# First MoE in eleven items of 384 tokens with singles and pairs between them

## The chip, the core and the metric

The kernel runs on one core of a Trainium2 chip, in one launch. The metric is the device time of one execution in microseconds. Three runs of the kernel before gave 1198.8, 1201.47 and 1198.43 us, a median of 1198.8. The engines are TensorE (PE; its weight loads PEld), VectorE (DVE), ScalarE (ACT), GpSimd (POOL) and SyncE (SP), which here issues most DMAs.

## The reference

Three steps follow one another: attention with keys and values averaged over groups of eight, a mixture of eight experts in which each of 4608 tokens goes to one of them, and a gated product without routing.

```python
scores = scale * np.matmul(q, k_p.transpose(0, 1, 3, 2))     # 8 x 8 heads, 576 queries, 72 pooled keys
x = softmax(scores) @ v_p                                    # as (4608, 512)
expert_idx = np.argmax(xn @ en.T / tau, axis=1)              # first MoE: one of E = 8 experts for a token
for e in range(E):
    mask = expert_idx == e
    h = np.maximum(x[mask] @ w1[e], 0.0)                     # 512 -> 1024
    out[mask] = gate_w[mask, None] * (h @ w2[e])             # 1024 -> 512
h = np.maximum(np.maximum(x @ m1, x @ m2), x @ m3)           # second MoE: 512 -> 768
return h @ mo                                                # 768 -> 512
```

The inputs are drawn with a fixed seed, so the routing is the same in every run.

## The kernel before

Attention takes the span up to about 166 us. The first MoE follows to 661 us. It sorts tokens by expert into blocks of 128, and works in *items*: a pair is two blocks of one expert, a single is one block. There are 18 pairs, of which the first `NE` are taken from the first 24 tiles of tokens while attention still runs, then the singles, of which four always run; more run only behind a branch on a number that the routing leaves in `nsing`. `run()` (L1525) goes through the items in turn, each in eight steps `p_`. Steps 0 to 3 are `mm1` (L1154): 256 of the 1024 hidden columns each, x times w1, with relu into `hhi` (ACT) and `hlo` (DVE). Steps 4 to 7 are `mm2` (L1191): the products with w2 gather in the four quarters of `py`. Every fp32 product is done as three matmuls of rounded parts: high x high, high x low, low x high. A weight piece, `w1raw` or `w2raw`, is split by `split()` two steps ahead of its use: ACT writes `whi`, DVE writes `wlo`; right after it the piece of the next item is loaded into the same buffer, skipped if the expert is the same. In mm1 a single takes fp32 products of 128 columns on unsplit weights; in mm2 its h is the stationary side, against 512 columns.

The next item's tokens are gathered by POOL into `xrow`, one indirect DMA for each block, in step 0. In step 5 `transpose_x` (L1112) turns them by TensorE into `px`, from where ACT copies `xhi` and DVE takes the rest as `xlo`. `px` comes from the pool `pq` with two PSUM banks. At the end of an item ACT copies `py` to `yo`, and SP stores it in `ybuf`.

Every engine takes its instructions in the order in which the program issues them. `between()` (L1564) is called twice in a step and issues, next to the item's own work, small steps of the routing (`fill`), then `conversions` (the raw weights of the second MoE turned to fp32 in `mraw`, through `cvraw` and `cvy`) and `combinations` (sums of weight blocks `wsum`, split into `wst`, stored by POOL to `wdram`, nine blocks in all), both mostly on DVE and ACT. The second MoE, from 661 us, reads these sums and works in groups of 768 tokens in the order of `ybuf`, with matmuls of 384 columns (L1901) on banks of PSUM.

The lines on which the order around the change rests:

```python
if p_ == 0 and i + 1 in items:
    gather(i + 1)
if p_ == 5 and i + 1 in items:
    transpose_x(i + 1)
```

## Time and profile before

| what | value |
|---|---|
| median of three runs | 1198.8 us |
| profiled execution, its own time | 1199.76 us |
| span of its trace | 1198.0 us |
| busy share of the span: TensorE, VectorE, ScalarE, GpSimd | 98%, 73%, 51%, 25% |
| DMA, mean over the span | 238 GB/s |

The span runs from the first to the last instruction in the trace. Busy time of TensorE counts overlapping matmuls once, and the end of a matmul is modelled: the time from one start to the next tells how fast it streams, better than the length of one. A wait is the idle time of an engine before an instruction, with the instruction that released it. [...]

### The profile page before, as it was taken

Reading aid. Unit: us, or ns where it says so; the run is one execution under the profiler, and the core shown is the slowest. Engines: PE = TensorE matmul, PEld = TensorE weight load, DVE = VectorE, ACT = ScalarE, POOL = GpSimd, SP = SyncE. Lnnn points to the kernel's source line nnn. Section 1 sums busy time; section 2 is a strip of 40 time slices with the busy share of each in tenths; the row PEclk is TensorE's granted clock in tenths of the full one; section 3 lists DMA queues with packets and bytes.
Section 4 is the critical chain, followed back from the end, with each engine's and each line's share of the span. In section 5 each row is a group of like instructions: output and inputs, shape, how many; then the busy total and the mean of one; then the engine's idle time right before and its main releaser. Section 6 shows DMA issues by size and latency. Waiting matters only on the chain.

```text
span 1198.0 us, 24005 instructions
## 1 busy us (share of the span) xinstructions
PE 1179.1 (98%) x8829; PEld 1165.6 (97%) x8829; DVE 876.7 (73%) x1811; ACT 607.2 (51%) x1117; POOL 302.9 (25%) x471
## 2 busy tenths in 40 slices
PE   8999999999999999999999999999999999999997
PEld 8999899999999999999999999999999999999997
DVE  7888977977899899988765468467557557567563
ACT  4676665455676666666655334334334334334332
POOL 8876843001212121221101202103004004004001
PEclk9999999999999999999999999999999999999999
DMA  9979665328865447554939677877878877877873
GB/s 287 314 194 257 182 213 189 102 24 262 269 230 201 148 169 248 208 194 141 323 130 330 224 258 294 313 261 285 314 261 284 299 283 279 293 298 276 288 258 137
DMA packets 106873, 285.12 MB, mean 238 GB/s; under 512 B 17798, under 2 KB 68148, under 8 KB 96380
## 3 DMA queue, kind: packets, MB, share of 16 engines
q1 hardware_dynamic: 87436, 217.60, 52.3%
q0 software_dynamic: 19312, 65.92, 17.4%
q8 instruction: 71, 1.16, 0.4%
q14 instruction: 54, 0.44, 0.1%
HBM read 285.52 MB, written 52.48 MB: 282 GB/s over the span
## 4 chain that ended last, share of the span: by engine, by line
PE 90%; DMA 4%; POOL 2%; DVE 1%; issue 1%; ACT 1%; SPq 0%; POOLq 0%
PE p L1901 33%; PE ph L1169 17%; PE py L1230 17%; PE o L2013 10%; PE pav L600 3%; PE ph L1177 2%; PE py L1214 2%; PE px L1123 1%; PE psc L538 1%; DMA vraw__727<-in_v_dram 1%; DMA qgrp<-in_q_dram 1%; DMA vraw__975<-in_v_dram 1%; PE paT L573 1%; PE pqT L512 1%; DMA kraw__141<-in_k_dram 0%
## 5 line engine op out<-in xcount | busy, mean ns | idle before, releaser
L1901 PE MATMUL p<-yhi,wt 128*128 128x384 f32 x1512 | 387.2, 336 | 0.1
L1901 PEld LDWEIGHTS p<-yhi,wt 128*128 128x128 f32 x1512 | 273.5, 188 | 0.3 <-issue 0.3
L1901 PE MATMUL p<-ylo,wt 128*128 128x384 f32 x756 | 254.1, 336 | 0.0
L1909 ACT COPY s<-p 128x384 f32<-128x384 f32 x162 | 77.6, 479 | 200.6 <-PE p L1901 200.6
L1230 PE MATMUL py<-hhi,whi 128*128 128x256 f32 x576 | 164.6, 286 | 0.0
L1169 PE MATMUL ph<-xhi,wlo 128*128 128x256 f32 x576 | 163.2, 283 | 0.5 <-DVE wlo L1149 0.5
L1169 PE MATMUL ph<-xhi,whi 128*128 128x256 f32 x576 | 163.6, 284 | 0.0
L1169 PE MATMUL ph<-xlo,whi 128*128 128x256 f32 x576 | 163.1, 283 | 0.0
L1230 PE MATMUL py<-hhi,wlo 128*128 128x256 f32 x576 | 163.0, 283 | 0.0
L1230 PE MATMUL py<-hlo,whi 128*128 128x256 f32 x576 | 163.0, 283 | 0.0
L1901 PEld LDWEIGHTS p<-ylo,wt 128*128 128x128 f32 x756 | 142.3, 188 | 0.0
L2013 PE MATMUL o<-wt,ghi 128*128 128x256 f32 x756 | 136.2, 282 | 0.0
L1928 DVE TENSOR_TENSOR blk<-p,s 128x384 f32<-128x384 f32 x108 | 59.7, 552 | 88.8 <-PE p L1901 88.8
L1886 POOL DMA_INDIRECT gt<-gbuf,ix x26 | 35.8, 1375 | 337.9 <-DMA ix<-idbuf 331.5
L2013 PEld LDWEIGHTS o<-wt,ghi 128*128 128x128 f32 x756 | 116.7, 188 | 0.9 <-DVE m L1929 0.2
L1169 PEld LDWEIGHTS ph<-xhi,wlo 128*128 128x128 f32 x576 | 110.6, 192 | 0.7 <-DVE wlo L1149 0.7
L1169 PEld LDWEIGHTS ph<-xhi,whi 128*128 128x128 f32 x576 | 110.6, 192 | 0.0
L1169 PEld LDWEIGHTS ph<-xlo,whi 128*128 128x128 f32 x576 | 110.6, 192 | 0.0
L1230 PEld LDWEIGHTS py<-hlo,whi 128*128 128x128 f32 x576 | 110.5, 192 | 0.0
L1230 PEld LDWEIGHTS py<-hhi,whi 128*128 128x128 f32 x576 | 110.5, 192 | 0.0
L1230 PEld LDWEIGHTS py<-hhi,wlo 128*128 128x128 f32 x576 | 110.5, 192 | 0.0
L1149 DVE TENSOR_TENSOR wlo<-w2raw,whi 128x1024 fp32r<-128x1024 f32 x86 | 105.1, 1226 | 6.9 <-ACT whi L1140 6.6
(384 smaller groups left out, 2361.5 us busy)
## 6 DMA issues: line engine op xcount, KB each, us to landing
wt<-wdram SPq DMA_DIRECT2D x69, 1792.0 KB
w1raw<-in_moe_w_dram SPq DMA_DIRECT2D x88, 512.0 KB
w2raw<-in_moe_w_dram SPq DMA_DIRECT2D x88, 512.0 KB
wdram<-wst POOLq DMA_DIRECT2D x9, 1792.0 KB, 6.7
ybuf<-yo SPq DMA_DIRECT2D x40, 256.0 KB
cvraw<-in_moe_w_dram POOLq DMA_DIRECT2D x36, 256.0 KB, 4.7
xbuf<-x SPq DMA_DIRECT2D x16, 512.0 KB
yr<-ybuf SPq DMA_DIRECT2D x20, 384.0 KB
```

The lines of the kernel that those rows point to most:

```text
L512: nc.tensor.transpose(ps[:, c * P : (c + 1) * P], blk_, ident)
L600: nc.tensor.matmul(ps[lo:hi, bank, (g0 % 4) * DA : (g0 % 4 + g1 - g0) * DA], aT[:, c, lo:hi], vbds[b % 3][:, sl : sl + g1 - g0, :].rearran ...
L1149: nc.vector.tensor_tensor(lo, src, hi.bitcast(F32), op=A.subtract)
L1169: nc.tensor.matmul(ps[:, f, :], a_[:, c, fs], b_[:, c, :], start=(n == 0), stop=(n == 3 * DC - 1))
L1177: nc.tensor.matmul(ps[:, f, 0:P], tl["w1"][piece][:, c, fs], xlo[:, c, 0:P], start=(c == 0), stop=(c == DC - 1))
L1214: nc.tensor.matmul(ps[h], a_[:, f, 0:P], b_[:, f, cols], start=(piece == 0 and f == 0 and n == 0), stop=(last_ and f == 1 and n == 2),)
L1230: nc.tensor.matmul(py[:, c // 2, (c % 2) * 256 : (c % 2 + 1) * 256], a_[:, f, c * P : (c + 1) * P], b_[:, f, :], start=(piece == 0 and f = ...
L1886: nc.gpsimd.indirect_dma_start(out=gt[g][:, j : j + 1], out_offset=None, in_=gbuf[:, :], in_offset=bass.IndirectOffsetOnAxis(ap=cols[j], a ...
L1901: nc.tensor.matmul(ps, a_, b_, start=(start and c + n == 0), stop=(c == 1 and n == 2), skip_group_check=True)
L1909: nc.scalar.copy(t, ps)
L1928: tt(src, add[0], add[1], op=A.add)
L2013: nc.tensor.matmul(ps, a_, b_, start=(m in (1, 2, 5) and c + n == 0), stop=(c == KH - 1 and n == 2), skip_group_check=True,)
```

## The change

The first MoE is cut another way. `TURN` lists the items: four early triples of 384 tokens, a fifth, then single, triple, pair, triple, single, triple, pair, and triples to the end, with a single as the last: 11 triples, 2 pairs, 3 singles, the same 40 blocks. Seven spare triples lie behind the branch, which then redoes the last three groups. An item of three blocks takes `px` in four tiles of 384 columns, in two halves: c = 0 and 1 in step 5, c = 2 and 3 in step 6, both through the two banks of `pq`. `py` has a bank for each of its four quarters. `yo` has four buffers, one for each quarter, each with its own store. `xrow`, `xhi` and `xlo` have one buffer each instead of two, `hT` four instead of five. A weight of the item behind a single is loaded once mm1 has read the piece before it, not in `split`. The steps of `conversions` and `combinations` are dealt out by new numbers, and `combinations` pauses twice where it paused once. POOL's four DMAs that filled the end of `ybuf` with ones are gone; SP has four that are skipped unless the branch is to be taken. The routing's small steps (`final_steps`) compute the new cut and are more than before.

```diff
-    NPAIR = 18
-    NSING = 8
-    NB = 2 * NPAIR + NSING
-    NITEM = NPAIR + NSING
-    NREQ = NPAIR + NSING // 2
+    NTRI, NPAIR, NSING, NMORE = 11, 2, 3, 7
+    NB3 = 3 * (NTRI + NMORE)
+    NB = NB3 + 2 * NPAIR + NSING
+    NREQ = NTRI + NPAIR + NSING
+    NITEM = NREQ + NMORE
+    assert NSING == NPAIR + 1
 
 
     CHK = [(0, 9), (9, 18), (18, 24), (24, 36)]
     NT1 = CHK[-1][0]
-    NE = -(-(NT1 * P - E * (2 * P - 1)) // (2 * P))
-    NBE = 2 * NE
+    NE = 4
+    NL = NTRI - NE
+    TURN = [*range(NE), 4, 11, 5, 12, 6, 13, 7, 14, 8, 9, 10, 15, *range(NREQ, NITEM)]
+    LATE = 13
...
-                tl["x"] = pool(stack, "xrow", 2)
+                tl["x"] = pool(stack, "xrow", 1)
 
             def open_c(stack=left):
-                tl["h"] = pool(stack, "hT", 5)
-                tl["y"] = pool(stack, "yo", 2)
+                tl["h"] = pool(stack, "hT", 4)
+                tl["y"] = pool(stack, "yo", 4)
...
-                return [2 * i, 2 * i + 1] if i < NPAIR else [NPAIR + i]
+                i = TURN[i]
+                if i < NTRI or i >= NREQ:
+                    b_ = 3 * i if i < NTRI else 3 * (NTRI + i - NREQ)
+                    return [b_, b_ + 1, b_ + 2]
+                k_, two = divmod(i - NTRI, 2)
+                b_ = NB3 + 3 * k_ + two
+                return [b_, b_ + 1] if two else [b_]
...
-                t = tl["x"].tile([P, 2, DM], F32, tag="xrow", name=f"xrow{i}")
+                t = tl["x"].tile([P, 3, DM], F32, tag="xrow", name=f"xrow{i}")
...
-            def transpose_x(i):
+            def transpose_x(i, half):
                 if i >= last[0]:
                     return
-                t = xrow.pop(i)
                 nblk = len(blocks(i))
-                hi = tl["x"].tile([P, DC, 256], F32R, tag="xhi", name=f"xhi{i}") if nblk == 2 else None
-                lo = tl["x"].tile([P, DC, 256], F32R if nblk == 2 else F32, tag="xlo", name=f"xlo{i}")
-                for c2 in range(2):
-                    ps = pq.tile([P, 512], F32, tag="pq", name=f"px{i}_{c2}").rearrange("p (c n) -> p c n", c=2)
-                    for c in range(2):
+                if half == 0:
+                    xT[i] = (
+                        tl["x"].tile([P, DC, 3 * P], F32R, tag="xhi", name=f"xhi{i}") if nblk > 1 else None,
+                        tl["x"].tile([P, DC, 3 * P], F32R if nblk > 1 else F32, tag="xlo", name=f"xlo{i}"),
+                    )
+                elif nblk < 3:
+                    return
+                t = xrow[i]
+                hi, lo = xT[i]
+                w_ = 1 if nblk == 3 else 2
+                apart = pb.tile([P, 2, 512], F32, tag="psc", name="px0_2") if i == 0 and half == 1 else None
+                done = []
+                for c0 in range(DC // 2 * half, DC // 2 * half + 2, w_) if nblk == 3 else (0, 2):
+                    ps = apart[:, c0 - 2, :] if apart is not None else pq.tile([P, 512], F32, tag="pq", name=f"px{i}_{c0}")
+                    ps = ps[:, 0 : w_ * nblk * P].rearrange("p (c n) -> p c n", c=w_)
+                    for c in range(w_):
                         for j in range(nblk):
                             nc.tensor.transpose(
-                                ps[:, c, j * P : (j + 1) * P], t[:, j, (2 * c2 + c) * P : (2 * c2 + c + 1) * P], ident
+                                ps[:, c, j * P : (j + 1) * P], t[:, j, (c0 + c) * P : (c0 + c + 1) * P], ident
                             )
-                    r = slice(2 * c2, 2 * c2 + 2)
-                    if nblk == 2:
-                        nc.scalar.copy(hi[:, r, :], ps)
-                        nc.vector.tensor_tensor(lo[:, r, :], ps, hi[:, r, :].bitcast(F32), op=A.subtract)
+                    done.append((ps, (slice(None), slice(c0, c0 + w_), slice(0, nblk * P))))
+                for ps, at_ in done:
+                    if nblk > 1:
+                        nc.scalar.copy(hi[at_], ps)
+                        nc.vector.tensor_tensor(lo[at_], ps, hi[at_].bitcast(F32), op=A.subtract)
                     else:
-                        nc.scalar.copy(lo[:, r, 0:P], ps[:, :, 0:P])
-                xT[i] = (hi, lo)
+                        nc.scalar.copy(lo[at_], ps)
...
-                    load_w(i + 1, piece)
+                    if len(blocks(i)) > 1 or piece > 5:
+                        load_w(i + 1, piece)
...
+                tag = ("pq", "psc", "paT", "pq")[piece] if i == 0 else ("psc", "pq")[piece % 2]
+                if tag == "pq":
+                    ps = [pq.tile([P, 512], F32, tag="pq", name=f"ph{i}_{piece}_{f}") for f in range(2 if nblk == 3 else 1)]
+                    whole_ = None
                 else:
-                    tag = ("psc", "", "paT", "psc")[piece] if i == 0 else ("psc", "pav")[piece % 2]
-                    ps = pb.tile([P, 2, 512], F32, tag=tag, name=f"ph{i}_{piece}")[:, 0, :]
-                ps = ps.rearrange("p (f n) -> p f n", f=2)
-                if nblk == 2:
+                    whole_ = pb.tile([P, 2, 512], F32, tag=tag, name=f"ph{i}_{piece}")
+                    ps = [whole_[:, f, :] for f in range(2)]
...
+                    for p_ in (3, 4, 5) if piece == 3 else (piece,):
+                        load_w(i + 1, p_)
...
-                    for k_ in range(2):
-                        yo = tl["y"].tile([P, 512], F32, tag="yo", name=f"yo{i}_{k_}")
-                        nc.scalar.copy(yo, py[:, k_, :])
-                        store_y(i, yo, 2 * k_, 2 * k_ + 2)
+                    for c in range(DC):
+                        yo = tl["y"].tile([P, 3 * P], F32, tag="yo", name=f"yo{i}_{c}")[:, 0 : nblk * P]
+                        nc.scalar.copy(yo, py3[c] if nblk == 3 else py[:, c // 2, (c % 2) * 256 : (c % 2 + 1) * 256])
+                        store_y(i, yo, c, c + 1)
...
+                    if i == NE and c0 == 0:
+                        vals["more"] = nc.sync.value_load(nsing[0:1, 0:1], min_val=0, max_val=NMORE)
+                        for c in range(DC):
+                            nc.sync.dma_start(
+                                ybuf[c * P : (c + 1) * P, N - 3 * GW : N].rearrange("p (a n) -> p a n", n=P),
+                                ones.unsqueeze(1).to_broadcast([P, 3 * GW // P, P]),
+                                cond=(vals["more"] != 0),
+                                bounds_check="skip_entire_dma",
+                            )
+                        nc.sync.dma_start(idbuf[:, 0 : NBE * P].rearrange("o (a p) -> (o a) p", p=P), idt[0:NBE, :])
...
-                        for _ in range(10):
-                            yield
+                        yield from pause(9)
...
-                transpose_x(items[0])
-                yield
+                for h in range(2):
+                    transpose_x(items[0], h)
+                    yield
...
-                    if p_ == 5 and i + 1 in items:
-                        transpose_x(i + 1)
+                    if p_ in (5, 6) and i + 1 in items:
+                        transpose_x(i + 1, p_ - 5)
...
-                    if half == 0:
-                        boundary(p_ in (0, 1, 2, 3, 7))
-                    fill(3)
-                elif i >= NPAIR - 1 and (i >= NPAIR or p_ > 5):
-                    for _ in range(((2, 2), (2, 1), (1, 0), (0, 0), (0, 0), (0, 1), (2, 2), (2, 2))[p_][half]):
+                    boundary(p_ in (4, 5, 6))
+                    fill(4)
+                nblk = len(blocks(i))
+                if i >= LATE:
+                    for _ in range(LAST[nblk][p_][half]):
                         next(cb, None)
                 else:
-                    for n in range(1 + (half and p_ % 2)):
-                        if next(cv, "end") == "end" and n:
-                            next(cb, None)
-                    next(cb, None)
+                    for _ in range((1 - half if nblk == 1 else 2 if half or (p_ % 2 and nblk == 3) else 1) if "slots" in ready else 0):
+                        next(cv, None)
+                    for _ in range(1 + (half and p_ % 2)):
+                        next(cb, None)
+
+            LAST = {
+                1: ((2, 2), (2, 1), (1, 0), (0, 0), (0, 0), (0, 1), (2, 2), (2, 2)),
+                3: ((2, 2), (2, 2), (2, 2), (1, 1), (2, 2), (2, 2), (2, 2), (2, 2)),
+            }
```

On TensorE, at the middle of a pair's mm2 in the first MoE, the kernel before has both tiles of the next item's x, then the products of w2:

```order
L1230 MATMUL py<-hhi_1_4481,wlo_5_4528 128x256
L1123 MATMUL px_0_4634<-ident,xrow_4443 128x128 x4
L1123 MATMUL px_1_4641<-ident,xrow_4443 128x128 x4
L1230 MATMUL py<-hhi_2_4520,whi_6_4565 128x256
L1230 MATMUL py<-hlo_2_4521,whi_6_4565 128x256
L1230 MATMUL py<-hhi_2_4520,wlo_6_4566 128x256
L1230 MATMUL py<-hhi_2_4520,whi_6_4565 128x256
```

At the first single between triples (item 5) the kernel after has two of four tiles, one step of six products with 512 columns, and the other two:

```order
L1188 MATMUL px_0_4831<-ident,xrow_4723 128x128 x3
L1188 MATMUL px_1_4835<-ident,xrow_4723 128x128 x3
L1283 MATMUL py_paT<-whi_6_4797,hhi_2_4763 128x512
L1283 MATMUL py_paT<-wlo_6_4798,hhi_2_4763 128x512
L1283 MATMUL py_paT<-whi_6_4797,hlo_2_4764 128x512
L1283 MATMUL py_paT<-whi_6_4797,hhi_2_4763 128x512
L1283 MATMUL py_paT<-wlo_6_4798,hhi_2_4763 128x512
L1283 MATMUL py_paT<-whi_6_4797,hlo_2_4764 128x512
L1188 MATMUL px_2_4864<-ident,xrow_4723 128x128 x3
L1188 MATMUL px_3_4868<-ident,xrow_4723 128x128 x3
L1283 MATMUL py_paT<-whi_7_4811,hhi_3_4785 128x512
```

The second pair of `px` tiles uses the banks of the first, and the step that separates them is the single's third one of mm2.

On VectorE, in the kernel before, in a pair, from the split of the sums (`wst`) and the conversions (`cvy`, `mraw`) to the first `xlo` of the next item:

```order
L1328 SCALAR_TENSOR_TENSOR cvy_4905<-cvraw_4777,cvy_4905 128x256
L1366 TENSOR_TENSOR wst_0_4869<-mraw_3909,wst_0_4869 128x512
L1330 SCALAR_TENSOR_TENSOR mraw_4903<-cvraw_4777,mraw_4903 128x256
L1369 TENSOR_TENSOR wst_0_4869<-mraw_3909,wst_0_4869 128x256
L1149 TENSOR_TENSOR wlo_7_4948<-w2raw_2526,whi_7_4947 128x1024
L1333 SCALAR_TENSOR_TENSOR mraw_4903<-cvy_4905,mraw_4903 128x256
L1371 TENSOR_TENSOR wst_0_4869<-wsum_0_4870,wst_0_4869 128x1024
L1312 TENSOR_SCALAR mraw_4903<-cvraw_4861 128x256
L1325 TENSOR_SCALAR cvy_4980<-cvraw_4861 128x256
L1129 TENSOR_TENSOR xlo_4983<-px_0_4984,xhi_4982 128x512
```

In the kernel after, in item 5, behind the last `hlo` of its mm1, up to the first `xlo` of the next item:

```order
L1444 TENSOR_TENSOR wsum_2_4790<-mraw_3495 128x256
L1445 TENSOR_TENSOR wsum_2_4790<-mraw_3495 128x256
L1448 TENSOR_TENSOR wsum_2_4790<-wsum_2_4790,mraw_3495 128x256
L1449 TENSOR_TENSOR wsum_2_4790<-mraw_3495,wsum_2_4790 128x256
L1214 TENSOR_TENSOR wlo_6_4798<-w2raw_2546,whi_6_4797 128x1024
L1410 SCALAR_TENSOR_TENSOR cvy_4771<-cvraw_4624,cvy_4771 128x256
L1452 TENSOR_TENSOR wst_2_4789<-mraw_3495,wst_2_4789 128x512
L1214 TENSOR_TENSOR wlo_7_4812<-w2raw_2547,whi_7_4811 128x1024
L1412 SCALAR_TENSOR_TENSOR mraw_4336<-cvraw_4624,mraw_4336 128x256
L1455 TENSOR_TENSOR wst_2_4789<-mraw_3495,wst_2_4789 128x256
L1457 TENSOR_TENSOR wst_2_4789<-wsum_2_4790,wst_2_4789 128x1024
L1195 TENSOR_TENSOR xlo_4830<-px_0_4831,xhi_4829 128x384
```

The sums, two splits of w2 and the conversions stand between a single's last `hlo` and the `xlo` that reads px_0.

## Rows read from the trace of the kernel before

**Rows 1.** The page's busy time of each engine over the span.

```profile
PE 1179.1 (98%) x8829; PEld 1165.6 (97%) x8829; DVE 876.7 (73%) x1811; ACT 607.2 (51%) x1117; POOL 302.9 (25%) x471
```

**Rows 2.** Waits of TensorE, 185 to 661 us: total, times, longest.

```profile
PE ph L1169 <- DVE wlo L1149: 0.5, 1, 0.5
PE pyT L1253 <- ACT yr L1222: 0.2, 1, 0.2
PE ph L1177 <- DVE hlo L1185: 0.2, 1, 0.2
```

**Rows 3.** Timeline of TensorE, 400 us: start, length, line, tiles, shapes, count.

```profile
399.75 0.28 PE L1169 MATMUL ph<-xhi,wlo 128*128 128x256 f32 x1
...
401.19 0.28 PE L1169 MATMUL ph<-xhi,wlo 128*128 128x256 f32 x1
```

**Rows 4.** Timeline of TensorE in the second MoE, 720 us.

```profile
719.94 0.34 PE L1901 MATMUL p<-ylo,wt 128*128 128x384 f32 x1
720.11 0.51 PE L1901 MATMUL p<-yhi,wt 128*128 128x384 f32 x2
720.46 0.34 PE L1901 MATMUL p<-ylo,wt 128*128 128x384 f32 x1
```

**Rows 5.** Windows: us, busy of PE, PEld, DVE, ACT, POOL, PEclk, DMA share, GB/s.

```profile
400.00:450.00 50.00, 50.00 (x421) 50.00 (x420) 46.72 (x89) 34.20 (x51) 10.45 (x15) 1.00 0.48 166
559.00:583.00 24.00, 24.00 (x203) 24.00 (x202) 18.93 (x26) 16.68 (x23) 8.04 (x12) 1.00 0.99 358
633.37:646.94 13.57, 13.57 (x98) 12.48 (x96) 6.33 (x8) 7.21 (x12) 0.00 (x0) 1.00 1.07 353
1190.00:1192.00 2.00, 1.28 (x11) 1.07 (x10) 0.97 (x2) 0.00 (x0) 0.98 (x1) 1.00 0.47 174
1194.00:1196.00 2.00, 0.00 (x0) 0.00 (x0) 0.00 (x0) 0.00 (x0) 0.00 (x0) 0.50 0.22 80
```

**Rows 6.** Tile px: ns min/median/max, first and last start; pair, first item.

```profile
L1123 PE MATMUL px<-ident,xrow x8: 272/272/273, 289.4 to 290.1; 128*128 128x128 f32 x8
...
L1123 PE MATMUL px<-ident,xrow x8: 272/273/273, 166.1 to 166.9; 128*128 128x128 f32 x8
```

**Rows 7.** Timeline of TensorE: first mm1 of two pairs, of two singles.

```profile
272.09 0.28 PE L1169 MATMUL ph<-xhi,whi 128*128 128x256 f32 x1
...
295.99 0.28 PE L1169 MATMUL ph<-xhi,whi 128*128 128x256 f32 x1
...
619.81 1.95 PE L1177 MATMUL ph<-xlo,w1raw 128*128 128x128 f32 x16
...
633.37 0.83 PE L1177 MATMUL ph<-xlo,w1raw 128*128 128x128 f32 x6
```

**Rows 8.** Groups of VectorE, 190 to 661 us: count, busy, mean ns, idle before.

```profile
L1149 DVE TENSOR_TENSOR wlo<-w2raw,whi 128x1024 fp32r<-128x1024 f32 x84 | 102.1, 1220 | 5.6 <-ACT whi L1140 5.2 <-DMA yr<-ybuf 0.2
...
L1333 DVE SCALAR_TENSOR_TENSOR mraw<-cvy,mraw 128x256 f32<-128x256 f32 x48 | 20.1, 418 | 0.0
...
L1371 DVE TENSOR_TENSOR wst<-wsum,wst 128x1024 fp32r<-128x1024 f32 x9 | 11.0, 1218 | 0.0
...
L1366 DVE TENSOR_TENSOR wst<-mraw,wst 128x512 fp32r<-128x512 f32 x9 | 6.2, 685 | 0.0
```

**Rows 9.** Timeline of VectorE in a single.

```profile
628.29 0.42 DVE L1185 SCALAR_TENSOR_TENSOR hlo<-ph,hhi 128x256 fp32r<-128x256 f32 x1
628.94 2.36 DVE L1149 TENSOR_TENSOR wlo<-w2raw,whi 128x1024 fp32r<-128x1024 f32 x2 [0.23 <-ACT whi L1140]
```

**Rows 10.** The page's costliest groups: 384 columns on VectorE.

```profile
L1928 DVE TENSOR_TENSOR blk<-p,s 128x384 f32<-128x384 f32 x108 | 59.7, 552 | 88.8 <-PE p L1901 88.8
```

**Rows 11.** Timeline of POOL at the first gathers, and their landing.

```profile
156.53 1.17 POOL L1102 DMA_INDIRECT xrow<-xbuf,idg  x1 [9.46 <-DVE rs L614]
158.00 1.04 POOL L1102 DMA_INDIRECT xrow<-xbuf,idg  x1 [0.30 <-DMA w1raw<-in_moe_w_dram]
...
DMA to landing us min/median/max: 6.1/6.3/6.3
```

More of the change, by code (lines that the diff above doesn't have):

```diff
@@ L647, in stage_x, with bank @@
                 return normalise
+            def bank(name):
+                if routed:
+                    return pb.tile([P, 2, 512], F32, tag="psc", name=name)[:, 0, :]
+                return pq.tile([P, 512], F32, tag="pq", name=name)
             def rt_(name, shape, dt=F32):
@@ L730, in rank_steps @@
                 yield "pe"
-                ps = pq.tile([P, 512], F32, tag="pq", name=f"prk{m}")
+                ps = bank(f"prk{m}")
                 fl = lambda a_: a_.rearrange("p t e -> p (t e)")
@@ L1132, in transpose_x @@
-                xT[i] = (hi, lo)
+                    done.append((ps, (slice(None), slice(c0, c0 + w_), slice(0, nblk * P))))
[3 more added lines that the diff above has]
+                        nc.vector.tensor_tensor(lo[at_], ps, hi[at_].bitcast(F32), op=A.subtract)
+                    else:
+                        nc.scalar.copy(lo[at_], ps)
             def split(i, piece):
                 src = w_raw(piece)
-                if not (i >= NPAIR and piece < 4):
+                if not (len(blocks(i)) == 1 and piece < 4):
@@ L1194, in mm2 @@
                 if "py" not in tl:
-                    tl["py"] = pb.tile([P, 2, 512], F32, tag="paT", name="py")
-                py = tl["py"]
+                    tl["py"] = [pb.tile([P, 2, 512], F32, tag=x_, name=f"py_{x_}") for x_ in ("paT", "pav")]
+                py, py3 = tl["py"][0], [t_[:, c, 0 : 3 * P] for t_ in tl["py"] for c in range(2)]
                 last_ = piece == 3
@@ L1336, in conversions, with pause @@
                     yield
-            mraw, whole, combined, last_pairs = [], [], [], []
+            mraw, whole, combined = [], [], []
+            def pause(n=2):
+                for _ in range(n):
+                    yield
             def combinations():
@@ L1532, in run @@
                     yield
-                transpose_x(items[0])
-                yield
+                for h in range(2):
+                    transpose_x(items[0], h)
+                    yield
                 for n, (i, p_) in enumerate(steps):
@@ L1656, in const_steps @@
                 yield
-                vs(gix2[:, 0 : NPAIR - NE, 0], iof[0:1, 0 : NPAIR - NE], 2.0, A.mult)
-                for s_ in range(0, NSING, 2):
-                    i0_ = NPAIR - NE + s_
-                    nc.vector.memset(gix2[:, i0_ : i0_ + 2, :], float(2 * (NPAIR - NE + s_ // 2)))
+                order = [b_ for i in range(NITEM) for b_ in blocks(i)]
+                turn_ = rt_("turn", [NB, NB])
+                tcol = rt_("tcol", [NB, 1])
+                b0 = 0
+                while b0 < NB:
+                    b1 = b0
+                    while b1 < NB and order.index(b1) - b1 == order.index(b0) - b0:
+                        b1 += 1
+                    vs(turn_[:, b0:b1], iof[0:NB, b0:b1], float(order.index(b0) - b0), A.add)
+                    b0 = b1
+                    yield
+                vv(sooner, turn_, ident[0:NB, 0:NB], A.mult)
+                yield
+                red(tcol, sooner)
+                yield
+                vs(sooner, turn_, tcol[:, 0:1], A.is_gt)
+                yield
+                n_ = NREQ - NE
+                nc.vector.memset(itri, 999.0)
+                nc.vector.tensor_copy(itri[:, 0:NL, 0], iof[0:1, 0:NL])
+                yield
+                nc.vector.tensor_copy(itri[:, n_:NI, 0], iof[0:1, NL : NL + NMORE])
+                vs(iblk[:, :, 0], itri[:, :, 0], 3.0, A.mult, float(NBE), A.add)
+                yield
+                vs(iblk[:, NL:n_:2, 0], iof[0:1, 0:NSING], 3.0, A.mult, float(NB3), A.add)
+                vs(iblk[:, NL + 1 : n_ : 2, 0], iof[0:1, 0:NPAIR], 3.0, A.mult, float(NB3 + 1), A.add)
                 yield
@@ L2101, in more @@
         gather(i0)
-        for _ in run(range(i0, i0 + 2), lambda half, p_, i: None):
+        for _ in run(range(i0, last[0]), lambda half, p_, i: None):
             pass
-        if i0 + 2 < NITEM:
-            with tc.If(need > i0 + 2 - NPAIR):
-                more(i0 + 2)
-    assert (NITEM - NREQ) * P <= GW
-    with tc.If(need > NREQ - NPAIR):
+        if last[0] < NITEM:
+            with tc.If(need > last[0] - NREQ):
+                more(last[0])
+    assert 18 * P <= 3 * GW
+    with tc.If(need > 0):
         with ExitStack() as st:
@@ L2120, in attention_moe_moe_kernel @@
         with ExitStack() as st:
-            second(st, [NG - 1], True)
+            second(st, list(range(NG - 3, NG)), True)
 _INS = [
```

303 lines of the change are left out of this document (167 added, 136 removed).

## The prediction, made before the changed kernel ran

> **What bounds the kernel now.** I read the busy shares first, then the waits of TensorE in the first MoE, then starts of its matmuls, and last the load of VectorE (DVE) in the same stretch. TensorE is busy 98% of the span [rows 1]. Between 185 and 661 us, where the first MoE lies, its waits come to 0.8 us in three places [rows 2]. So that stage is a stream of matmuls, and its length is their number times the distance between two starts. That distance is what the change touches: 256-column matmuls start 0.12 us apart, twelve of them in 1.44 us [rows 3]; 384-column ones, in the second MoE of the same kernel, start three in 0.52 us, 173.4 ns each [rows 4]. A column thus costs 0.469 ns at 256 and 0.452 ns at 384. The second thing to see is DVE: 46.72 of 50 us between 400 and 450 [rows 5]. It hides behind TensorE now, with little to spare, and the change shortens the stretches that it hides behind.
>
> **A. The stream.** A pair of 256 tokens has 96 matmuls in each of its two products, 192 x 0.120 = 23.04 us, and 8 transposes of x at about 0.1 us [rows 6]; 23.83 us, and the trace has 295.99 - 272.09 = 23.90 [rows 7]. A single takes 633.37 - 619.81 = 13.56 [rows 7]. A triple of 384 tokens has 192 x 0.1734 = 33.29 us and 12 transposes, 34.47 us. Before: 18 x 23.90 + 4 x 13.56 = 484.4. After: 11 x 34.47 + 2 x 23.90 + 3 x 13.56 = 467.7. Term: **-16.8 us**. Of it 15.2 come from 33 blocks that cost 11.49 us in a triple instead of 11.95 in a pair, and 1.6 from one single that becomes part of a wider item.
>
> [...]
>
> **B. DVE at the two singles between triples (items 5 and 9).** This is the step that I expect to cost most. Before, an item's x is transposed in one step into both banks of `px`, two steps of mm2 before it is wanted. After, it comes in halves, a step apart: px_0 and px_1 fill the two banks, and px_2 waits until DVE has read px_0 into xlo. Behind a single, the step between is six 512-column matmuls, about 1.4 us, where a pair has 24 x 0.12 = 2.9 and a triple 24 x 0.1734 = 4.2. DVE runs in order, and ahead of that xlo stand a whole block of weight sums, two weight splits and conversion steps, as the order's rows show: after hlo_3 four operations of 256 columns on wsum, two wlo, three more of 256 columns, one of 512, one of 1024. At 0.42, 1.22, 0.69 and 1.22 us [rows 8] that is 7 x 0.42 + 2 x 1.22 + 0.69 + 1.22 = 7.3 us, less some 0.08 each where instructions overlap (two wlo in 2.36 us, [rows 9]): 6.5 us, and 0.5 more for the xlo itself, by the 384-column row [rows 10]. In a single of before hlo_3 starts at 628.29, 8.5 us after the item's start [rows 7, 9], and ends at 8.9; so px_0 is free at 15.4 to 16. TensorE is at px_2 after four products of mm1 (7.5 us), three of mm2 (4.2) and the first half's transposes (0.6): 12.3. It waits 3.1 to 3.7 us there, and another 0.5 after it for the split that stands behind the xlo. I take **+4.0 for each, +8.0**. From below it is 0: DVE drained its queue in every stretch of before without a TensorE wait [rows 2]. From above it is 6.5 each: every operation ahead of xlo is also held up by ACT's casts and the weight store whose buffer they wait for. I take 4.0, as all of it but the overlap is in rows.
>
> **C. The pairs between triples (items 7 and 11).** The same bank, with a step of 2.9 us between the halves' place and the next item: the block of sums stands earlier there in DVE's order, and I count 1.8 and 0.5 us late: **+2.3**, from 0 to 5.
>
> **D. The start.** The first item's x comes by three gathers instead of two. They go out 1.47 us apart on POOL (156.53, 158.00) and land 6.3 us later [rows 11], so the third lands at about 159.5 + 6.3 = 165.8, just when the first transpose starts now (166.1, [rows 6]). I take **+1.0** for the later half and the longer chain of small routing steps on DVE; 0 to 4.
>
> **E. The clock.** [...] I take **+1.0** for two, 0 to 5, low because only the longest waits would get there. [...]
>
> **At nothing:** 44 weight splits fewer on DVE and ACT (1.22 us each on DVE), hidden now and so no gain on the path, though they leave DVE idle inside triples; four stores of y for each item instead of two, on SP, with four buffers, so no copy waits; the four skipped DMAs behind item 4 and the load of group 0's tokens on SP, which have the whole of the item's successor to pass; POOL's four stores of ones, gone from a queue that nobody waited for; the branch on spare items, read where it was read. hT goes from five buffers to four: mm2 of a piece frees one before the next item's mm1 asks. If a store of y were late, its next copy would hold py and cost TensorE directly; 0.2 MB is too little for that.
>
> **Sum:** -16.8 + 8.0 + 2.3 + 1.0 + 1.0 = -4.5 us. The profiled run took 1199.76 us by its own time (span 1198.0), so it would be 1195.3; the median of the runs is 1198.8, 1.0 lower, and 1194.3 with it.
>
> **Rivals.**
> 1. DVE keeps up. Triples leave it long idle stretches, so it may enter the single with nothing behind it, and rows 2 show no wait at a 93% load. Then B, C and E are 0: 1198.8 - 16.8 + 1.0 = 1183. Against it: the load inside the 13.6 us of a single is some 17 us, which no earlier idleness pays for, since the order fixes it there. Chance 0.16.
> 2. The waits eat all. B at 6.5 each, C at 3, D and E near 2 make 18 - 16.8: 1198 to 1200. For it: the block of sums also waits for the store of the one before it. Chance 0.16.
> 3. Slower: late weights behind a single. Each of items 5 to 11 brings in another expert than the one before, 4.2 MB. Inside one single the DMA has to move these, 0.8 MB of gathers and 0.8 of y, 0.5 of raw conversions and 1.8 of weight sums, 8.1 MB; at the 353 to 358 GB/s that the busiest stretches show [rows 5] that takes 22.8 us, 9.3 more than the single lasts. If the weights come last of these, TensorE waits up to 9.3 us at each of the two, instead of B: -16.8 + 18.6 + 2.3 + 2.0 = +6, 1205. It is slower than before once a wait passes about 8 us. Against it: a single of before brings in its 4.2 MB at 353 GB/s in 13.57 us with no wait [rows 2, 5], and splits ask for the pieces one after another, the last well inside the next triple. Chance 0.12.
> 4. 384 columns gain nothing here: distance 1.5 x 0.12 = 0.18 us, as a stream without any fixed cost would have it, so A is -1.6 and the waits of B to E stay: 1198.8 - 1.6 + 12.3 = 1209.5. Rows 4 are against it. Chance 0.03. [...]
> 5. The change does not do what it says: routing wants more than the 16 items, and the branch redoes three groups. Counted from the reference's inputs, the experts have 42, 708, 1, 145, 0, 2242, 1018 and 452 tokens, 42, 621, 1, 145, 0, 1666, 145 and 452 of them in the first 24 tiles; they fill 11 triples, 2 pairs and 3 singles exactly. A hundred us and more if I counted wrongly. Chance 0.01.
>
> **How the numbers follow.** The forecast has 0.52, its own range 1190 to 1199 by the bounds of B and C about their middle. A measurement of this kernel tells 0.3%, 3.6 us, from no change: faster is below 1195.2, slower above 1202.4. Faster: all of rival 1 and two thirds of the forecast, 0.50. Same: the rest of the forecast, 0.17, and nearly all of rival 2, 0.15: 0.32. Slower: 0.18. The range takes in rival 1 below, and above it reaches between rival 2 and rival 3: 1182.5 to 1203.
>
> **What would show it.** In the changed kernel the PE waits should name px of the triple behind items 5 and 9, released by DVE's xlo, 3 to 4 us each, and less behind 7 and 11. Triples should start 34.5 us apart, their matmuls 0.173 us. The second stage's first matmul should stand near 656 us against 661.43. The granted clock tells E. A wait on w1raw or on whi in items 6 and 10 would speak for rival 3; no px waits at all, for rival 1. I am wrong if triples are slower than 34.5 us without a wait, or if the time is lost outside the first MoE.

## The result, and the profile after

The changed kernel takes 1211.78 us, the median of four runs (1208.43 to 1216.04), against 1198.66 for the kernel before. The ratio is 1.0106, 95% interval [1.0069, 1.0142]: some 13 us slower, where I had forecast 4.5 us faster and given 1203 as the upper end. The profiled execution took 1210.62 us (span 1208.8), 10.9 more than that of before, and the working below is against it.

The second MoE starts 8.45 us later, at 669.88 against 661.43. Here are the first matmuls of items 5 to 12 and of the second MoE in the changed kernel, to be read as [rows 7]: the third to fifth columns are engine, line and operation, and a single is the line with w1raw.

```profile
349.98 0.27 PE L1248 MATMUL ph<-xlo,w1raw 128*128 128x128 f32 x1
...
370.42 0.34 PE L1240 MATMUL ph<-xhi,whi 128*128 128x384 f32 x1
...
405.08 0.28 PE L1240 MATMUL ph<-xhi,whi 128*128 128x256 f32 x1
...
436.34 0.34 PE L1240 MATMUL ph<-xhi,whi 128*128 128x384 f32 x1
...
470.07 0.27 PE L1248 MATMUL ph<-xlo,w1raw 128*128 128x128 f32 x1
...
489.28 0.33 PE L1240 MATMUL ph<-xhi,whi 128*128 128x384 f32 x1
...
523.94 0.28 PE L1240 MATMUL ph<-xhi,whi 128*128 128x256 f32 x1
...
552.15 0.34 PE L1240 MATMUL ph<-xhi,whi 128*128 128x384 f32 x1
...
669.88 0.45 PE L2002 MATMUL p<-yhi,wt 128*128 128x384 f32 x1 [0.73 <-ACT yo L1327]
```

From start to start the first single takes 370.42 - 349.98 = 20.44 us and the second 19.21, where the singles of before took 13.56. The pairs take 31.26 and 28.21, where those of before took 23.90. The triples behind them take 34.66 each (405.08 - 370.42), close to the 34.47 worked out in term A. So the triples do nearly what they should, and the four narrow items between them do not. The waits of TensorE between 200 and 669 us, which were 0.9 us in all from 185 on [rows 2], are now these (in total, times, longest), with one of 0.2 us more behind the last item:

```profile
PE px L1188 <- DVE xlo L1195: 7.1, 3, 2.9
PE px L1188 <- DMA xrow<-xbuf,idg: 3.3, 2, 2.3
PE py_paT L1300 <- DVE wlo L1214: 2.6, 1, 2.6
PE py_paT L1283 <- DVE wlo L1214: 0.5, 1, 0.5
PE ph L1240 <- DVE hlo L1259: 0.3, 1, 0.3
```

All five kinds lie in the four narrow items and add up to 13.9 us before rounding. In an undisturbed run of the same items, below, a single takes 14.02 us and a pair 24.30. The four items are therefore 6.4, 7.0, 5.2 and 3.9 us too long, 22.5 in all, and the waits explain only 13.9 of it. What the rest is, the windows of the changed kernel show (columns as in [rows 5]; PEclk, the granted clock of TensorE as a share of full speed, is the third from the end):

```profile
362.00:364.00 2.00, 0.16 (x1) 0.16 (x2) 2.00 (x5) 0.00 (x0) 0.05 (x1) 0.67 1.02 354
364.00:366.00 2.00, 2.00 (x7) 1.75 (x8) 2.00 (x3) 1.48 (x3) 1.09 (x2) 0.50 1.10 360
366.00:368.00 2.00, 2.00 (x8) 1.57 (x7) 1.61 (x3) 0.42 (x1) 0.00 (x0) 0.50 1.06 380
...
428.00:430.00 2.00, 1.87 (x9) 1.58 (x8) 1.97 (x5) 0.83 (x1) 0.00 (x0) 0.50 0.86 282
...
486.00:488.00 2.00, 2.00 (x9) 1.81 (x8) 2.00 (x5) 1.29 (x3) 0.21 (x1) 0.50 1.13 423
546.00:548.00 2.00, 0.00 (x0) 0.00 (x0) 1.97 (x5) 1.67 (x3) 0.26 (x1) 1.00 0.00 0
```

TensorE is busy from 364 to 368 with a granted clock of 0.50, where it was 1.00 up to 362. The timeline of the first single shows the same in the pace of the products:

```profile
359.90 0.27 PE L1188 MATMUL px<-ident,xrow 128*128 128x128 f32 x1
361.25 0.33 PE L1188 MATMUL px<-ident,xrow 128*128 128x128 f32 x1 [1.08 <-DMA xrow<-xbuf,idg]
363.84 1.12 PE L1188 MATMUL px<-ident,xrow 128*128 128x128 f32 x4 [2.26 <-DMA xrow<-xbuf,idg]
365.19 0.63 PE L1283 MATMUL py_paT<-wlo,hhi 128*128 128x512 f32 x1
365.61 0.63 PE L1283 MATMUL py_paT<-whi,hlo 128*128 128x512 f32 x1
```

TensorE stood for 1.08 and then 2.26 us at the second and third block of px_0, for x that the gather had not yet brought, and the 512-column products behind it start 0.42 us apart instead of the 0.23 ahead of the wait. Such a fall follows the waits in three of the four items; the windows at 428 and 486 are from the first pair and the second single. At the second pair a wait of 2.9 us left the clock at 1.00 (546 to 548), and there only 0.7 us beside the waits is lost. At the other three it is 6.4 - 3.3, 7.0 - 4.1 and 5.2 - 3.2, together 7.9 us before rounding.

The waits have three different origins. At the first single it is the gather. POOL's timeline, and the time to landing of the three gathers:

```profile
352.20 0.54 POOL L1378 DMA_DIRECT2D cvraw<-in_moe_w_dram  x1 [3.53 <-DVE mraw L1412]
353.04 1.07 POOL L1157 DMA_INDIRECT xrow<-xbuf,idg  x1 [0.30 <-issue]
...
355.74 1.45 POOL L1157 DMA_INDIRECT xrow<-xbuf,idg  x1 [0.30 <-issue]
...
DMA to landing us min/median/max: 6.2/6.8/8.1
```

The gather goes out 3 us into the single, behind a load of raw weights whose buffer VectorE frees late, in three pieces, and lands 6 to 8 us behind each issue; a single asks for x 9.9 us after it began. In the pairs it is the raw weights of the second MoE. VectorE in the first pair:

```profile
424.53 0.29 DVE L1394 TENSOR_SCALAR mraw<-cvraw 128x256 int32<-128x256 int32 x1 [4.76 <-DMA cvraw<-in_moe_w_dram]
424.74 1.22 DVE L1214 TENSOR_TENSOR wlo<-w2raw,whi 128x1024 fp32r<-128x1024 f32 x1
```

It stands 4.76 us for cvraw, and the split wlo for TensorE's next product is queued behind. POOL had issued that load as the second of these two, behind a store of weight sums:

```profile
413.58 0.58 POOL L1458 DMA_DIRECT2D wdram<-wst  x1 [1.16 <-DVE wst L1457]
414.25 0.56 POOL L1378 DMA_DIRECT2D cvraw<-in_moe_w_dram  x1
```

It was used 10.3 us after that, at 424.53. In the second pair the load that VectorE stands for, 3.37 us, also went out right behind a store of weight sums, and landed 7.5 us later; the median of all these loads in the first MoE is 5.6 us here, and 4.2 us in the kernel before. Over the whole stage this idle time before the first conversion step was 4.9 us in the kernel before, and is 19.8 us now (count, busy, mean, then idle and what ended it); first before, then after:

```profile
L1312 DVE TENSOR_SCALAR mraw<-cvraw 128x256 int32<-128x256 int32 x48 | 13.7, 286 | 4.9 <-DMA cvraw<-in_moe_w_dram 3.5 <-DMA cvraw<-in_moe_w_out_dram 1.5
```

```profile
L1394 DVE TENSOR_SCALAR mraw<-cvraw 128x256 int32<-128x256 int32 x48 | 13.9, 290 | 19.8 <-DMA cvraw<-in_moe_w_dram 13.2 <-DMA cvraw<-in_moe_w_out_dram 6.5
```

At the second single it is what I had predicted, VectorE's queue: the splits, the conversions and the block of sums end at 485, and only then come the two xlo that free the banks.

```profile
482.54 1.22 DVE L1214 TENSOR_TENSOR wlo<-w2raw,whi 128x1024 fp32r<-128x1024 f32 x1
...
483.88 1.22 DVE L1457 TENSOR_TENSOR wst<-wsum,wst 128x1024 fp32r<-128x1024 f32 x1
485.01 1.01 DVE L1195 TENSOR_TENSOR xlo<-px,xhi 128x384 fp32r<-128x384 f32 x2
```

Beside the first MoE, the second takes 538.9 us instead of 536.6. Two of its six stretches of 384-column products take 65.8 and 65.7 us instead of 64.5.

### The profile page after: what moved, and what is told of

It reads as the page before. It is cut to its first block, busy times and chain, and to the rows that moved or that the text cites. A ratio compares the mean times of both kernels' runs of the same rounds, so it can differ in the third digit from the quotient of the medians.

```text
span 1208.8 us, 21565 instructions
## 1 busy us (share of the span) xinstructions
PE 1175.8 (97%) x7777; PEld 1159.8 (96%) x7777; DVE 836.5 (69%) x1814; ACT 563.6 (47%) x1100; POOL 302.4 (25%) x467
## 4 chain that ended last, share of the span: by engine, by line
PE 80%; DVE 7%; DMA 6%; issue 3%; POOL 2%; ACT 1%; SPq 0%; POOLq 0%; ACTq 0%; DVEq 0%
PE p L2002 33%; PE ph L1240 14%; PE o L2114 10%; PE py_paT L1300 7%; PE py_pav L1300 6%; PE pav L604 3%; PE psc L542 2%; DVE wlo L1214 1%; DMA cvraw<-in_moe_w_dram 1%; DMA cvraw<-in_moe_w_out_dram 1%; PE px L1188 1%; DMA vraw__731<-in_v_dram 1%; DMA vraw__979<-in_v_dram 1%; PE paT L577 1%; PE ph L1248 1%
## 5 line engine op out<-in xcount | busy, mean ns | idle before, releaser
L1240 PE MATMUL ph<-xhi,whi 128*128 128x384 f32 (+1 forms) x416 | 136.4, 328 | 0.3 <-DVE hlo L1259 0.3
L1240 PE MATMUL ph<-xlo,whi 128*128 128x384 f32 (+1 forms) x416 | 135.8, 326 | 0.2 <-DVE xlo L1195 0.2
L1240 PE MATMUL ph<-xhi,wlo 128*128 128x384 f32 (+1 forms) x416 | 135.8, 326 | 0.0
L2114 PE MATMUL o<-wt,glo 128*128 128x256 f32 x378 | 106.8, 283 | 0.0
L1258 ACT ACTIVATE hhi<-ph 128x384 fp32r<-128x384 f32 (+3 forms) x86 | 48.9, 569 | 82.8 <-PE ph L1240 74.3
L1259 DVE SCALAR_TENSOR_TENSOR hlo<-ph,hhi 128x384 fp32r<-128x384 f32 (+3 forms) x86 | 54.8, 648 | 46.4 <-ACT hhi L1258 46.0
L1300 PE MATMUL py_paT<-hhi,wlo 128*128 128x384 f32 (+1 forms) x240 | 77.9, 325 | 2.6 <-DVE wlo L1214 2.6
L1300 PE MATMUL py_paT<-hhi,whi 128*128 128x384 f32 (+1 forms) x240 | 79.8, 333 | 0.0
L1240 PEld LDWEIGHTS ph<-xhi,wlo 128*128 128x128 f32 x416 | 78.3, 188 | 0.0
L1300 PE MATMUL py_paT<-hlo,whi 128*128 128x384 f32 (+1 forms) x240 | 77.8, 324 | 0.0
```

The source lines that it names most:

```text
L1240: nc.tensor.matmul(ps[f][:, 0:cols], a_[:, c, fs], b_[:, c, 0:cols], start=(n == 0), stop=(n == 3 * DC - 1))
L1258: nc.scalar.activation(h_, src, AF.Relu)
L1259: nc.vector.scalar_tensor_tensor(lo[:, f_, 0:cols], src, 0.0, h_.bitcast(F32), A.max, A.subtract)
L1300: nc.tensor.matmul(py3[c] if nblk == 3 else py[:, c // 2, (c % 2) * 256 : (c % 2 + 1) * 256], a_[:, f, c * P : (c + 1) * P], b_[:, f, 0 : ...
L2114: nc.tensor.matmul(ps, a_, b_, start=(m in (1, 2, 5) and c + n == 0), stop=(c == KH - 1 and n == 2), skip_group_check=True,)
```

## The experiments

Three theories went in. A: the loss is TensorE's waits at the narrow items, each with a fall of the clock behind it. B: the triples or the weights of the next expert are slow as such. C: narrow items cost the same in any order. The variants start from the changed kernel. The ratio is to the kernel before, with its 95% interval.

**All triples first, then pairs, then singles.**

```diff
-    TURN = [*range(NE), 4, 11, 5, 12, 6, 13, 7, 14, 8, 9, 10, 15, ...]
+    TURN = [*range(NE), 4, 5, 6, 7, 8, 9, 10, 12, 14, 11, 13, 15, ...]
-                    for _ in range(1 + (half and p_ % 2)):
+                    for _ in range(2 if nblk == 2 else 1 + (half and p_ % 2)):
                         next(cb, None)
```

> The same 16 items as in the changed kernel, but in another order: all 11 triples first, then the two pairs, then the three singles, with two steps of the weight sums in each half step of the pairs. Theory A (the time is lost as TensorE waits at the four narrow items that have a triple behind them, and each such wait lets the granted clock fall): no narrow item has a triple behind it any more, so the 13.9 us of waits and some 8 us at the lower clock go; about 1211.8 - 21 = 1190 us, granted clock 1.00 up to the second MoE. Theory B (triples themselves bring less than the stream promises, through late weights or slower second MoE): the time stays within 4 us of 1212. Theory C (the order only moves the waits into the row of singles, where each brings in another expert): 1198 to 1206.

Measured: 1198.0 us, ratio 0.9986 [0.9973, 0.9999]; 13.8 us better than the changed kernel, and 8 short of theory A's 1190. No triple waits any more, but my denser steps had brought the preparation of the second MoE's first rows forward (its loads go out at 580.95, ten us earlier than in the same order without those steps, below), and in the last pair ACT stood 6.0 and VectorE 7.0 us for its DMAs. That gave TensorE one wait of 7.2 us, and the clock was at 0.50 to 0.52 from 592 to 602 (waits, then windows). Theory C's number, 1198 to 1206, is touched, but not by its mechanism: the row of singles has under 2 us of waits.

```profile
PE ph L1240 <- DVE hlo L1259: 7.2, 1, 7.2
```

```profile
592.00:594.00 2.00, 0.00 (x0) 0.00 (x0) 1.21 (x3) 0.81 (x1) 0.00 (x0) 0.50 0.63 176
598.00:600.00 2.00, 2.00 (x11) 2.00 (x11) 2.00 (x5) 2.00 (x5) 0.00 (x0) 0.50 0.99 331
```

**The second half of px in other banks.**

```diff
-                apart = pb.tile(..., tag="psc", name="px0_2") if i == 0 and half == 1 else None
+                apart = pb.tile(..., tag="psc", name=f"px{i}_2") if half == 1 else None
```

> The changed kernel, with the second half of the x transposes of every triple in the PSUM banks psc, which are free there, instead of in the two banks of the first half. Theory A: the waits of px for xlo (7.1 us in three places) go, with half of the clock loss, so 1211.8 - 7 - 4 = about 1201; the waits for the gather (3.3) and for wlo behind the raw conversions (2.6) stay. Rival: VectorE's queue is late as a whole, so the same wait turns up at the next triple's first mm1, which needs xlo and wlo from the same queue, and the time stays within 3 us of 1212.

Measured: 1216.25 us, ratio 1.0152 [1.0122, 1.0182], 4.5 us worse. Theory A failed, and the rival's mechanism held, though its number (within 3 us of 1212) was missed by 1.5 us: the wait moved to the next item's mm1, and became longer, while 2.7 us of waits for the gather stayed.

```profile
PE ph L1240 <- DVE xlo L1195: 12.7, 4, 4.0
```

So the bank is where the wait of the changed kernel shows, not what causes it; the cause is that xlo is late in VectorE's queue.

**The gather one item earlier.**

```diff
-                    if p_ == 0 and i + 1 in items:
+                    if n == 0 and i + 1 in items:
                         gather(i + 1)
                     if p_ in (5, 6) and i + 1 in items:
                         transpose_x(i + 1, p_ - 5)
+                    if p_ == 6 and i + 2 in items:
+                        gather(i + 2)
```

> The changed kernel, with the gather of an item's tokens issued one item earlier, right behind the transposes that free its buffer. Theory A: of the waits only the one for the gather goes, at the first single (3.3 us, and some 3 us of the clock fall behind it): about 1205 to 1206. Rival: behind the gather VectorE's queue is late there as well, as at the second single, and the wait changes its name only: 1209 to 1212.

Measured: 1206.95 us, ratio 1.0077 [1.0052, 1.0101]. The number is near theory A's, but not for its reason. The first single is as long as before (20.60 us): the gather is in time, and VectorE's queue is next. The gain came in the other three items, each 1.1 to 2.8 us shorter. The second single has the same waits as in the changed kernel (0.5 and 2.65 us), but the clock stays at 1.00 behind them, and it takes 17.79 us instead of 19.21. The longest wait of the first single, then the window behind the wait of the second:

```profile
PE px L1188 <- DVE xlo L1195: 2.9, 1, 2.9
```

```profile
486.00:488.00 2.00, 2.00 (x12) 1.78 (x11) 2.00 (x5) 2.00 (x5) 1.56 (x2) 1.00 1.11 441
```

**A slower pace of conversions in pairs.**

```diff
-                    for _ in range((1 - half if nblk == 1 else 2 if half or (p_ % 2 and nblk == 3) else 1) if "slots" in ready else 0):
+                    for _ in range((1 - half if nblk == 1 else 2 if nblk == 3 and (half or p_ % 2) else 1) if "slots" in ready else 0):
                         next(cv, None)
```

> The changed kernel, with 2 instead of 3 steps of the raw conversions in each step of a pair, so that the load of the raw weights has 8.6 instead of 5.8 us. Theory A: VectorE no longer stands still for the raw weights in the two pairs (4.8 and 3.4 us), so the waits there go (2.6 + 1.5 and 2.9 us, with some 3 us of the clock): about 1211.8 - 10 = 1202. Rival (the DMA is what is late, whatever the pace): VectorE still stands for the raw weights and the time stays within 3 us of 1212.

Measured: 1201.62 us, ratio 1.0018 [1.0006, 1.0031]: 10.2 us better. That is the number expected, and VectorE no longer stands for the raw weights in either pair, but only one pair is freed. The second takes 24.32 us, an undisturbed one. The first takes 27.49: 2.8 us of wait for xlo, and 0.4 us besides. The waits for the gather are those of the two singles:

```profile
PE px L1188 <- DMA xrow<-xbuf,idg: 5.6, 4, 2.8
PE px L1188 <- DVE xlo L1195: 2.8, 1, 2.8
```

What holds the first pair now is a store of weight sums, issued at 412.62: ACT stands for its buffer, and the splits and xlo queue behind.

```profile
422.93 0.62 ACT L1446 CAST wst<-mraw 128x512 fp32r<-128x512 f32 x1 [4.83 <-DMA wdram<-wst]
```

**No conversions and no weight sums in the singles**, more weight sums in triples, what is left of the conversions in the last items, and the pairs at the slower pace; once with the gathers where they were, once with the early ones.

```diff
                 if i >= LATE:
+                    next(cv, None)
...
-                else:
-                    for _ in range((1 - half if nblk == 1 else 2 if half or (p_ % 2 and nblk == 3) else 1) if "slots" in ready else 0):
+                elif nblk > 1:
+                    for _ in range((2 if nblk == 3 and (half or p_ % 2) else 1) if "slots" in ready else 0):
                         next(cv, None)
-                    for _ in range(1 + (half and p_ % 2)):
+                    for _ in range(1 + half if nblk == 3 else 1 + (half and p_ % 2)):
                         next(cb, None)
```

> As the run with the steps held out of singles, but with the gathers where the changed kernel has them. Theory A: gathers are issued on POOL behind loads of raw weights whose buffers VectorE frees late; with no conversion in the single the gather goes out 3.5 us earlier but still lands some 8 us behind its issue, 2 us late at most: 1189 to 1194. If the gather were late by its own transfer, its 3.3 us and 3 us of clock stay at both singles: 1196 to 1200.

> The changed kernel in its own order of items, with no conversion and no weight-sum step in the singles between triples, the slower conversion pace in pairs, what is left of the conversions dealt out in the last items, more weight-sum steps in triples, and each gather one item earlier. Theory A (waits at the four narrow items, doubled by the clock): all four waits have lost their releaser, so TensorE streams through and the clock stays at 1.00: 1211.8 - 13.9 - 8 - some = 1187 to 1191, faster than before. Rival (late weights behind a single, since each narrow item reloads 4.2 MB whatever VectorE does): new waits for whi or w1raw in the items behind the singles, 1196 to 1202.

Measured: 1190.69 us, ratio 0.9931 [0.9916, 0.9946], and 1190.96, ratio 0.9934 [0.9921, 0.9948]. Both are faster than the kernel before in the changed kernel's own order of items, by some 8 us, and both lie in the range of theory A. First matmuls of the first single, the triple and the pair behind it, and the second MoE, with the gathers where they were:

```profile
348.06 0.27 PE L1248 MATMUL ph<-xlo,w1raw 128*128 128x128 f32 x1
...
362.08 0.34 PE L1240 MATMUL ph<-xhi,whi 128*128 128x384 f32 x1
...
396.74 0.28 PE L1240 MATMUL ph<-xhi,whi 128*128 128x256 f32 x1
...
421.04 0.34 PE L1240 MATMUL ph<-xhi,whi 128*128 128x384 f32 x1
...
647.40 0.69 PE L2003 MATMUL p<-yhi,wt 128*128 128x384 f32 x1 [0.74 <-ACT yo L1327]
```

The single takes 14.02 us and the pair 24.30, while the same weights are reloaded: theory B is out, and so is my rival 3. The gather needs no earlier place once POOL is not held up by a raw-weight load. It goes out 2.0 us before the single begins instead of 3.1 us into it, and takes no less time to land (6.9 to 8.3 us behind each issue): its lateness came from the queue ahead of it. These runs change several things at once (steps out of the singles, the pace in pairs, more sums in triples), so they show that the side work was the cause, not what each part of it cost.

**The order of the first run with the changed kernel's weight-sum steps, and the slower pace in pairs.**

> All triples first, then pairs, then singles, with the changed kernel's own weight-sum steps (not the denser ones of the earlier order run) and 2 conversion steps in each step of a pair. Theory A: the one wait of 7.2 us of the earlier order run, for the second MoE's first rows of y, came from its denser steps and goes with its 4 us of lower clock: 1198 - 11 = 1187. Rival: without triples behind them, pairs and singles still have too little time for the next expert's weights, and the wait comes back in another place: 1194 to 1199.

Measured: 1188.84 us, ratio 0.9915 [0.9902, 0.9929], some 10 us faster than the kernel before and the lowest median here, though not clear of the two runs above. Both pairs are undisturbed (23.90 and 23.47 us); which of the two edits freed them is not separated. The second MoE starts at 649.18. The waits of TensorE from 200 us to there:

```profile
PE py_paT L1283 <- DVE wlo L1214: 1.4, 3, 0.8
PE pyT L1322 <- ACT yr L1292: 0.2, 1, 0.2
```

**Products that nobody reads, in the place of the waits.** They change no output; they only keep TensorE at work.

```diff
+                        for _ in range({(5, 1): 13, (9, 2): 11}.get((i, piece), 0)):
+                            nc.tensor.matmul(tl["py"][1][:, 0, :], hhi[:, 0, 0:P], whi[:, 0, :], ...)
```

> The changed kernel, with products that nobody reads in the place of the waits: 13 of 512 columns (3.0 us) before px_0 of the first single, 11 (2.5 us) before px_2 of the second, into a bank that is free. Theory A with the clock as a cost of its own: TensorE is late there anyway, so the added work costs nothing, and the clock does not fall; the two singles take 17.3 and 17.0 us instead of 20.4 and 19.2, and the time is 1211.8 - 5 = 1206 to 1207. Rival (the products at the lower clock lose nothing, since they would wait for VectorE anyway): the singles take as long as before or longer, 1211 to 1214.

Measured: 1207.11 us, ratio 1.0065 [1.0049, 1.008], 4.7 us better than the changed kernel, with 24 matmuls more. The singles take 17.91 and 17.78 us instead of 20.44 and 19.21. The pairs, which the edit leaves alone, still wait 4.1 us each, and the mean granted clock of the execution is 0.996, against 0.990 in the changed kernel. Timeline of the first single, then a window:

```profile
359.37 3.12 PE L1291 MATMUL py_pav<-whi,hhi 128*128 128x512 f32 x13
362.32 0.38 PE L1188 MATMUL px<-ident,xrow 128*128 128x128 f32 x2
363.32 0.66 PE L1188 MATMUL px<-ident,xrow 128*128 128x128 f32 x4 [0.62 <-DMA xrow<-xbuf,idg]
```

```profile
364.00:366.00 2.00, 2.00 (x13) 1.50 (x13) 2.00 (x4) 1.77 (x4) 0.57 (x2) 1.00 1.09 368
```

The wait at px shrinks to 0.62 us and the clock is 1.00 where it was 0.50. That separates the two costs: the waits alone are not the loss; in the changed kernel the clock behind them is a third of it (7.9 of 22.5 us).

**Both kernels once more.**

> The kernel before once more, for its second MoE alone. In the traces so far each stretch of 384-column products there takes 64.5 us or some 65.7; the kernel before had none of the long kind, the changed kernel two, its variants none to three. If that is chance from one execution to the next, before shows one or two of the long kind here as well, and its other parts repeat to 0.3 us. If the change makes them, before has none again.

> The changed kernel once more, unchanged. By chance the long stretches of the second MoE lie in other places or are fewer than two; if the change makes them they are the first and the fifth again. Theory A on the first MoE: the same four places lose time again, 20 to 24 us over an undisturbed stream, but with other shares of gather, raw weights and queue, since which of them is last depends on where transfers fall.

Measured, one run each: 1199.73 and 1211.96 us. The kernel before repeated to 0.1 us in every item and again had no long stretch in the second MoE. The changed kernel lost 7.0, 6.1, 5.2 and 6.0 us at the four narrow items, 24.3 in all, and had one long stretch, the first. Its waits in these items come to 14.5 us. At its second pair one wait of 2.8 us was followed by a granted clock of 0.50 (550 to 552, below), and the pair took 30.30 us; in the first execution a wait of 2.9 us there left the clock at 1.00, and the pair took 28.21.

```profile
550.00:552.00 2.00, 2.00 (x11) 2.00 (x10) 1.69 (x5) 1.91 (x4) 1.56 (x2) 0.50 0.13 16
```

So the length of a wait alone does not tell here whether the clock falls: behind 2.8 us it fell, behind 2.9 it did not. What decides it, these runs do not show.

## Why the prediction was wrong

**A, the stream: right in kind, 0.2 us too short for a triple.** Triples run at 34.65 us against 34.47 worked out, just over the 34.5 that I had named as a sign of being wrong. (The waits of [rows 2] add up to 0.9 us, not the 0.8 that I read; nothing hangs on it.) The run with all triples first starts the second MoE 12.3 us earlier than before. The other 4.5 of the 16.8 expected are some 0.9 in the first items, beside the end of attention, 1.0 in the other triples, and 2.6 in its row of singles, which take 14.3, 14.6 and 15.3 us.

**B, the singles: size near, cause half right.** I had 4.0 us of waits at each; 3.3 and 3.2 came. At the second it was VectorE's queue ahead of xlo, as worked out: TensorE came to px_2 12.9 us into the item, for 12.3 forecast, and px_0 was free at 15.5, for 15.4 to 16. At the first the gather was later still. I had asked when the first gather of the kernel lands, and not when one lands that is issued inside a 14 us item behind another DMA on POOL. With the gather early the queue's own waits stood there instead, 2.9 us at px and 1.5 at the splits behind it.

**C, the pairs: failed.** 2.3 us forecast, 4.1 + 3.3 = 7.4 us of waits came, and not mainly from the block of sums ahead of xlo that I had counted. The step that failed is one that I left out: the raw conversions at the pairs stood at nothing. The new pacing deals out three of their steps in each step of a pair, 24 in an item instead of 20: with two cvraw buffers a load has six steps to land, 5.8 us instead of 7.2, and VectorE stands for it with TensorE's splits behind it. I named the change of pace nowhere, and so priced it at nothing. Nor did I price the landing: the two loads that were waited for took 10.3 and 7.5 us, behind a store of weight sums, which is more than the old pace allowed as well. How the 7.4 us divide between pace and landing is open. The slower pace, 8.6 us, freed the second pair; in the first the store itself then held ACT, as my upper bound for B had it.

**E, the clock: failed in size.** I took 1.0 us, with 5 as the upper end; 7.9 came. This is the largest single error. The step that failed is "low because only the longest waits would get there": at the first pair, which I had not counted, the clock was at 0.50 from 428 to 434, behind a wait of 2.6 us, and the three falls cost 2.0 to 3.1 us each. The 0.5 us that I took for each was my own estimate, and no run shows it. By the windows of 2 us the clock was at 0.50 for some 3 to 7 us each time.

**D, the start: near, but not shown.** The first mm1 starts at 170.11 against 169.28, 0.8 us for 1.0. In the variants, whose start is the same but for the gathers of two of them, it lies between 168.2 and 170.9, so this agreement is luck as much as anything.

**Rivals.** Rival 2, all of the gain eaten, had the right direction, but 18 us for all of B to E, where some 22.6 came. Rival 3 named the DMA but the wrong transfer: it was the gather and the raw weights, not the next expert's, and items 6 and 10 have no wait at all. Rival 4's 1209.5 us lies nearest to the measured time, by luck: its triples would take 35.7 us. With A as forecast and the others as measured, the sum is -16.8 + 13.9 + 7.9 + 0.8 + 2.3 in the second MoE = 8.1 us, of 10.9. The other 2.8 are smaller pieces: about 1.7 as the narrow items take 14.02 and 24.30 us even undisturbed, not 13.56 and 23.90; 0.7, the rest of the second pair; 0.9 and 0.6 in the first and last items; less 1.3 in the triples, of which those ahead of a narrow item take 33.7 us.

## What to carry to other kernels

When items shrink, what is dealt out beside them has to shrink with them: work out for the narrowest item the queue of each in-order engine, the landing of each transfer issued in it, and the depth of every ring of buffers that its pace uses, for a busy share over 50 us tells nothing of that. In this kernel waits of two to three microseconds of TensorE were followed in some items by 2.0 to 3.1 us of loss in clock: 13.9 us of waits cost 22.5 in one execution and 14.5 cost 24.3 in another. An estimate from these two is some 1.6 to 1.7 times the length of the waits, for a plan that trades some streaming for a few of them. Changing where a wait shows moved it (other banks; at the first single an earlier gather); taking the side work out of the narrow items ended it.

## What the runs showed beside

The stretches of 384-column products in the second MoE take 64.5 us or some 65.7, never a value between. One of 66.1, in the run with the steps held out of singles, came behind waits of 1.2 and 0.7 us at the end of the first MoE. The kernel before had none of the long kind in two profiled executions, the changed kernel two and one, its variants none to three, not always in the same places; from 669.88 to 734, in a long one, the granted clock was 1.00. The instructions are the same. I did not find what makes them, so up to 3.7 us of a comparison of two executions may be theirs.
